# The next block's third and fourth W1 sums behind the second result of the block ahead

## The chip, the cores and the metric

The kernel runs on one core of one Trainium2 chip. What counts is the time of one execution on the device in microseconds (us). A core has five engines that run side by side, each working through its own instructions in their written order: PE (matrix products), DVE (elementwise work on vectors), ACT (activations and copies), POOL (here it mostly issues indirect DMAs, which gather and scatter rows) and SP (issues the plain DMAs). They wait for one another through semaphores.

## The reference

Attention over a causal window of 64 positions, then a mixture of experts in which each token goes through one expert's two matrix products.

```
B, H, S, D, E, F = 8, 8, 576, 512, 8, 1024      # D = 8 heads of 64
x = softmax(q k^T / 8 inside the window) v      # heads joined: (8, 576, 512)
logits = x @ w_gate;  local = sigmoid(x @ w_local)
for every sequence b, token s:
    e = argmax(logits) if s == 0 or local < 0.5 else the token before's e
    out[b, s] = softmax(logits[b, s])[e] * (relu(x[b, s] @ w1[e]) @ w2[e])
```

Everything is in 32-bit floats; there are 4608 tokens.

## The kernel before, in words

The first third computes attention and the gate. Then the tokens are sorted by expert into blocks, and the blocks are worked through one after another by `Experts.run`. A large block has 256 rows of one expert; the rows left over go into blocks of 128, 64 or 32 rows. The fixed order is: three early large blocks (-1, -2, -3), then 0, 1, a 128-row block, 2, a 32-row block, 3, a 128-row block, 4, 5, a 128-row block, 6, a 32-row block, 7, a 128-row block, 8, 9, a 64-row block, 10, 11, 12, and a last 64-row block.

From block -3 on, a large block's two matrix products (x by W1 in `big_hidden`, the result h by W2 in `big_result`) are each made as seven products of quarter matrices instead of eight, by Winograd's scheme. That takes sums of quarters ahead of the products: four sums of the left operand (`left`), four of the right one (`right`). For the first matrix product the left operand is W1 (tile `ws`, four sums of 128x1024 elements) and the right one x (tile `xs`). For the second it is h (`hs`) and W2 (again shown as `ws`). All of these sums run on DVE. In `left`, sum 2 needs sum 1, sum 4 needs sum 2, and sum 3 needs neither of them.

I number the seven products of a `big_result` R1 to R7 and those of a `big_hidden` H1 to H7, in the order in which PE runs them. Their PSUM tiles (`hp`) come from a pool of three buffers, and each product waits for whoever still reads its buffer. After R4, R5 and R6, DVE makes a quarter of the result from PSUM (`put`, line 1419). I call them the first, second and third put. The last quarter, after R7, is made by ACT. R7 adds onto the PSUM tile that the second put reads (`px`), so PE may not begin R7 before the second put has ended. H1 of the next block uses the buffer that the first put reads, and H2 the one that the third put reads.

In `run`, while PE is at R1 to R7 of one block, the DVE work for the next block has been written ahead of the puts: `turn` transposes the gathered rows, and `prepare` makes the four `xs` and the four W1 sums. H2 uses W1 sum 1, H3 sum 2, H5 sum 3 and H6 sum 4. In the stage this case is about, engines DVE, ACT, POOL, PE and SP all follow the written order. The hooks passed to `big_result` are called between the products; `step`, which most of them hold, has nothing left to do once the router's work is over, which is so before the places that change.

The third put is followed by the W2 sums of the next block (line 1320, written into a single buffer, so they wait for R7, which still reads the old ones), and on POOL by the scatter of the first half of the result (line 1488), behind which POOL has gathers for later blocks (line 1184). SP loads a block's W1 and W2 (line 1261) into a ring of four buffers, once PE and DVE are done with the old contents.

Of the kernel before, what the change touches and what calls it, by code (L numbers as in the profile page):

```python
# [42 lines left out]
FB = 3  # L43
# [131 lines left out]
def attention(ctx, tc, ring, kq, v3, v4, vt, vh, xs, lt, ok, wg, wg2, ident, rt, ex, small):  # L175
# [303 lines left out]
    for i, (sc, hp) in enumerate(units):  # L479
# [18 lines left out]
        if hp == 3 and sc not in GATED:  # L498
            turn(sc, x, 0)
            old = x  # L500
        elif sc and sc - 1 not in GATED:
            if hp == 0:
                turn(sc - 1, old, 1)
            elif hp == 2:
                logits(sc - 1, turned)
# [207 lines left out]
class Router:  # L713
# [70 lines left out]
    @staticmethod  # L784
    def last(ap):
        return ap.rearrange("p (c o) -> p c o", o=1)
# [5 lines left out]
    def gate(self, part, psum):  # L792
# [36 lines left out]
        for i in range(2):  # L829
# [55 lines left out]
                               Alu.add, Alu.add)  # L885
        base = tl("base", P, E * CMAX)[:, :E * n].rearrange("p (e c) -> p e c", e=E)
        vec.tensor_tensor(base, run, te, op=Alu.subtract)
        yield 1.9 if part else 1.2, False
        cnt = self.cnt[part]
# [270 lines left out]
def quarters(t, rows, cols):  # L1160

    r, c = rows // 2, cols // 2
    return [[t[:, i * r:(i + 1) * r, j * c:(j + 1) * c] for j in range(2)] for i in range(2)]


class Experts:
# [98 lines left out]
    def begin(self):  # L1265
        self.jobs = [self.fetch(-1)]

    def turn(self, st, quiet, later=False):
        while any(x is st for x, _ in self.asks):
            self.ask()  # L1270
        nc, n = self.nc, st["rows"]
        a = slice(HF, HF + n) if "quarter" in st else slice(n)
        st["xt"] = xt = self.xtp.tile([P, DK, BIG], F32, name="xt")
        for i, x in enumerate(st["x"]):
            o = xt[:, :, i * P:(i + 1) * P]
            if st["plain"]:
                tp = self.ps_t.tile([P, DK, P], F32, name="tp")
                for kk in range(DK):
                    nc.tensor.transpose(tp[:, kk, :n], x[a, kk * P:(kk + 1) * P], self.ident[a, a])
                (nc.scalar.copy if quiet else nc.vector.tensor_copy)(o[:, :, :n], tp[:, :, :n])  # L1280
                continue
            first, parts = st["parts"][0], len(st["parts"])
            nc.vector.transpose(
                o[:, :, :n].rearrange("p j (m t) -> p m j t", m=parts),
                x[:, first * P:(first + parts) * P].rearrange("p (m j d) -> p m j d", m=parts, j=DK))
        if n < P:
            pws = st["pw"][0]
            st["pw"] = pw = self.wk.tile([P, 1], F32, name="pw")
            for i in range(P // n):
                nc.vector.tensor_copy(pw[i * n:(i + 1) * n], pws[a])  # L1290
        if st["fast1"] and not quiet and not later:
            self.prepare(st)

    def prepare(self, st):

        st["xq"] = quarters(st["xt"], DK, BIG)
        st["xt"] = self.right("xs", st["xq"])
        w = quarters(st["w1"], DK, F)

        st["wq"] = [[w[0][0], w[1][0]], [w[0][1], w[1][1]]]  # L1300
        st["ws"] = self.left("ws1", st["wq"])

    def left(self, name, a):

        sub, add = Alu.subtract, Alu.add
        s1, s2, s3, s4 = self.sums(name, a)
        for o, x, y, op in ((s1, a[1][0], a[1][1], add), (s2, s1, a[0][0], sub), (s3, a[0][0], a[1][0], sub),
                            (s4, a[0][1], s2, sub)):
            self.nc.vector.tensor_tensor(o, x, y, op=op)
        return s1, s2, s3, s4  # L1310

    def right(self, name, b, marks=()):

# [18 lines left out]
    def halves(self, st):  # L1332

        hq = st["hq"]
        st["ha"] = [[hq[0][0], hq[1][0]], [hq[0][1], hq[1][1]]]
        st["hs"] = self.left("hs", st["ha"])

    def big_hidden(self, st, step):

# [244 lines left out]
    def run(self, ctx, rt, last=None):  # L1584

        tc = self.tc
        self.space(ctx)
        ps_r = ctx.enter_context(tc.tile_pool(name="ex_ps_r", bufs=1, space=PSUM))
        ctx.enter_context(tc.manual_schedule(engines={ET.PE, ET.SP}))
        rt.rows_of(ctx, tc, "rt_oh2", 3)  # L1590
        jobs = self.jobs

        def psum():
            return ps_r.tile([P, SC], F32, name="r")

        side = rt.second(psum)
        pause = 0.0

        def step():
            nonlocal side, pause  # L1600
            pause, trip = max(pause - STEP, -1.5), False
            while side and not trip and pause <= 0.0:
                w, trip = next(side, (0.0, None))
                pause += w + (0.6 if trip else 0.0)
                if trip is None:
                    side = None

        order = [-1 - n for n in range(FB)]
        between = [*range(NB, NB + SURE[1]), *range(KINDS[1] + 1, KINDS[1] + SURE[2])]
        quarters = list(range(KINDS[2], KINDS[2] + SURE[3]))  # L1610
        for n in range(SURE[0]):
            order.append(n)
            if n % 2 and between:
                order.append(between.pop(0))
            elif n % 4 == 2 and quarters:
                order.append(quarters.pop(0))
        order += between
        order.append(KINDS[1])
        assert not quarters
        jobs += [self.rows({}, order[1])] + [{"plain": True} for _ in range(2, FB)]  # L1620
        jobs[FB - 2]["later"] = True
        held = self.one.tile([1, 1], F32, name="held")
        self.nc.sync.dma_start(out=held, in_=jobs[1]["x"][1][:1, :1])
        for i, n in enumerate(order[1:FB]):
            self.weights(jobs[1 + i], n)
        self.turn(jobs[0], True)
        step()
        pause += 3.4
        for i, n in enumerate(order):
            quiet = i < FB  # L1630
            if i == FB - 1:
                while side and not rt.ready:
                    step()
                mark = last(self.ps_y.tile([P, D], F32, name="yp")) if last else None

                ctx.enter_context(tc.manual_schedule(engines={ET.PE, ET.SP, ET.DVE, ET.Activation, ET.Pool}))
                jobs.append(self.weights(self.rows({}, order[FB], True, True), order[FB]))
                jobs.append(self.weights({"plain": False}, order[FB + 1]))
                if jobs[i]["fast1"]:
                    self.prepare(jobs[i])  # L1640
            elif i >= FB:
                if i + 2 < len(order):
                    self.weights(jobs[i + 2], order[i + 2])
                if i + 3 < len(order):
                    jobs.append(self.rows({}, order[i + 3], paced=True))
            self.flush()
            if FB - 1 <= i < len(order) - 1:
                jobs[i]["later"] = True
            if n >= KINDS[2]:
                continue  # L1650
            if i == 1:
                pause += 4.5
            with tc.issue_after(mark.ins) if i == FB - 1 and mark else nullcontext():
                self.hidden(jobs[i], quiet, step, ((FK - 1, lambda: rt.links), (FK - 3, lambda: rt.links))[i] if i < 2 else None)
            if i + 2 < FB:
                self.rows(jobs[i + 2], order[i + 2], paced=True)
            if i == 1:
                rt.behind = jobs[1]["last"]
            if i == FB - 1:
                while side:  # L1660
                    step()
                self.rows(jobs[FB + 1], order[FB + 1], paced=True)
                jobs.append(self.rows({}, order[FB + 2], paced=True))
            if i + 1 == len(order):
                self.result(jobs[i], step)
                continue
            self.turn(jobs[i + 1], i + 1 < FB)
            if i + 2 < FB and jobs[i + 1]["fast1"]:
                self.prepare(jobs[i + 1])
            hooks = (step, ) * 6  # L1670
            if order[i + 1] >= KINDS[2]:
                one, turned, two = self.quarter(jobs[i + 1])
                after = jobs[i + 2]
                hooks = (lambda: None), one, turned, two, (lambda: self.turn(after, False, True)), \
                    (lambda: self.prepare(after))
            self.result(jobs[i], step, hooks)
# [64 lines left out]
```

## Time and profile before

| what | value |
|---|---|
| median of 3 runs | 633.9 us (629.37 to 635.15) |
| the profiled execution | 631.83 us, its span 630.1 us |
| PE busy | 604.0 us (96%) |
| DVE busy | 402.1 us (64%) |
| POOL busy | 275.5 us (44%) |
| ACT busy | 200.7 us (32%) |
| PE's waits for a put (line 1419) | 2.0 us in 6 waits |

The trace gives each instruction's start and length on its engine, and before an idle stretch the instruction that ended it. PE's matmuls are pipelined, so one starts before the former has ended; the distance from one start to the next is what a product takes.

### The profile page before, as it was taken

Reading aid. Unit: us, or ns where it says so; the run is one execution under the profiler, and the core shown is the slowest. Engines: PE = TensorE matmul, PEld = TensorE weight load, DVE = VectorE, ACT = ScalarE, POOL = GpSimd, SP = SyncE. Lnnn points to the kernel's source line nnn. Section 1 sums busy time; section 2 is a strip of 40 time slices with the busy share of each in tenths; the row PEclk is TensorE's granted clock in tenths of the full one; section 3 lists DMA queues with packets and bytes.
Section 4 is the critical chain, followed back from the end, with each engine's and each line's share of the span. In section 5 each row is a group of like instructions: output and inputs, shape, how many; then the busy total and the mean of one; then the engine's idle time right before and its main releaser. Section 6 shows DMA issues by size and latency. Waiting matters only on the chain. (4 is left out here: it accounts for less than half of the span.)

```text
span 630.1 us, 15072 instructions
## 1 busy us (share of the span) xinstructions
PE 604.0 (96%) x6253; PEld 530.7 (84%) x6253; DVE 402.1 (64%) x757; ACT 200.7 (32%) x368; POOL 275.5 (44%) x261
## 2 busy tenths in 40 slices
PE   8897988999999999999999999999999999999995
PEld 7676766788889998979898889888997998989994
DVE  5667569888986867346472785183927753886730
ACT  3756655632482131203130213022211221213120
POOL 4532111532103567448165873174375765462001
PEclk9999999999999999999999999999999999999998
DMA  8999898886945566487966765678678656965501
GB/s 319 397 419 400 326 377 298 287 319 238 384 154 202 185 227 250 165 295 248 403 244 236 304 221 208 225 305 318 284 262 320 225 186 240 374 217 208 197 18 39
DMA packets 31880, 165.80 MB, mean 263 GB/s; under 512 B 10531, under 2 KB 12217, under 8 KB 22586
## 3 DMA queue, kind: packets, MB, share of 16 engines
q1 hardware_dynamic: 20394, 135.54, 57.9%
q0 software_dynamic: 11408, 29.20, 13.0%
q8 instruction: 51, 0.84, 0.5%
q14 instruction: 27, 0.22, 0.1%
HBM read 145.52 MB, written 19.59 MB: 262 GB/s over the span
## 5 line engine op out<-in xcount | busy, mean ns | idle before, releaser
L1184 POOL DMA_INDIRECT xg<-xs,g x118 | 139.1, 1179 | 46.5 <-issue 25.6
L1488 POOL DMA_INDIRECT out_dram<-y,idx x36 | 40.8, 1133 | 159.0 <-DVE y L1419 69.9
L1408 PE MATMUL hp<-ws,hs 128*128 128x256 f32 x384 | 88.9, 380 | 0.0
L1408 PEld LDWEIGHTS hp<-ws,hs 128*128 128x128 f32 x384 | 72.6, 190 | 10.9 <-issue 1.2
L1357 PE MATMUL hp<-xs,ws 128*128 128x128 f32 x672 | 79.7, 275 | 0.0
L1357 PEld LDWEIGHTS hp<-xs,ws 128*128 128x128 f32 x672 | 77.3, 192 | 0.1
L1508 PE MATMUL hp<-xt,w 128*64 128x64 f32 (+2 forms) x640 | 66.2, 276 | 0.0
L1508 PEld LDWEIGHTS hp<-xt,w 128*128 128x128 f32 (+1 forms) x640 | 60.8, 170 | 4.1 <-issue 0.7
L1419 DVE SCALAR_TENSOR_TENSOR y<-hp,pws,kept 128x256 f32<-128x256 f32 x48 | 22.1, 480 | 63.5 <-issue 38.1
L1408 PE MATMUL hp<-w,h 128*128 128x256 f32 x256 | 60.5, 379 | 0.0
L1369 DVE TENSOR_TENSOR h<-hp,keep 128x512 f32<-128x512 f32 x42 | 28.6, 690 | 44.0 <-PE hp L1357 43.2
L1357 PEld LDWEIGHTS hp<-xt,w 128*128 128x128 f32 x448 | 53.2, 192 | 2.7 <-issue 2.3
L1357 PE MATMUL hp<-xt,w 128*128 128x128 f32 x448 | 54.7, 275 | 0.0
L394 PEld LDWEIGHTS sp<-w 64*64 64x64 f32 x1296 | 39.9, 139 | 16.1 <-issue 11.5
L1408 PEld LDWEIGHTS hp<-w,h 128*128 128x128 f32 x256 | 47.3, 190 | 5.7
L394 PE MATMUL sp<-w 64*64 64x128 f32 (+1 forms) x1296 | 45.8, 272 | 5.7 <-issue 4.2
L425 ACT ACTIVATE p<-sp 128x512 f32<-128x512 f32 x72 | 39.1, 595 | 37.6 <-PE sp L394 35.2
L440 PE MATMUL xo<-vb,p 128*64 128x74 f32 (+1 forms) x576 | 45.0, 230 | 5.5 <-DVE x L450 2.2
L430 DVE TENSOR_TENSOR p<-p,mask 128x1024 f32<-128x1024 f32 x29 | 35.6, 1227 | 22.6 <-ACT p L425 22.5
L1184 POOL DMA_INDIRECT pws<-xw,gx x40 | 43.7, 1093 | 13.1 <-issue 9.8
L440 PEld LDWEIGHTS xo<-vb,p 128*64 128x64 f32 x576 | 39.2, 139 | 9.7 <-issue 4.0
L1320 DVE TENSOR_TENSOR ws<-w 128x1024 f32<-128x1024 f32 x32 | 39.1, 1224 | 11.5 <-PE hp L1408 9.6
(287 smaller groups left out, 967.3 us busy)
## 6 DMA issues: line engine op xcount, KB each, us to landing
w<-in_w_dram SPq DMA_DIRECT2D x22, 2048.0 KB, 9.4
w<-in_w1t_dram SPq DMA_DIRECT2D x20, 2048.0 KB, 8.9
w<-in_kq_dram SPq DMA_DIRECT2D x17, 1024.0 KB, 10.4
w<-in_w_dram SPq DMA_DIRECT2D x24, 512.0 KB, 8.3
xs<-x POOLq DMA_DIRECT2D x9, 1024.0 KB, 7.0
va<-in_v_dram SPq DMA_DIRECT2D x5, 1184.0 KB, 5.3
vtt<-in_vt_dram SPq DMA_DIRECT2D x5, 1024.0 KB, 6.3
va<-in_v_dram SPq DMA_DIRECT2D x3, 1040.0 KB, 14.2
```

Of the source, the lines that this page charges most:

```text
L394: nc.tensor.matmul(sp[j][c * WIN:(c + 1) * WIN, a:b], lhsT=kt[h, hp, block * WIN:(block + 1) * WIN], rhs=qt[h, hp, a:b], start=not biased, ...
L425: nc.scalar.activation(p[:, j], sp[j], Act.Exp, scale=DH ** -0.5)
L430: masked.append(nc.vector.tensor_tensor(p, p, m.to_broadcast([P, 2, SC]), op=Alu.mult))
L440: nc.tensor.matmul(xo[par * WIN:(par + 1) * WIN, j, s * VW:s * VW + n], lhsT=p[:, j, b * WIN:(b + 1) * WIN], rhs=w[:, s, 2 * hp + j, :n], ...
L1184: return self.nc.gpsimd.indirect_dma_start(out=out, out_offset=None, in_=table[:rows, :], in_offset=bass.IndirectOffsetOnAxis(ap=idx, axis=0))
L1320: self.nc.vector.tensor_tensor(o, x, y, op=sub)
L1357: mm = nc.tensor.matmul(out[:, m, :], lhsT=a[:, kk, m * P:(m + 1) * P], rhs=b[:, kk, :], start=start and m + kk == 0, stop=stop and (m, kk ...
L1369: nc.vector.tensor_tensor(o, x, y, op=add)
L1408: mm = nc.tensor.matmul(out, lhsT=a[:, m, :], rhs=b[:, m, :], start=start and m == 0, stop=stop and m == FK // 2 - 1, skip_group_check=True)
L1419: nc.vector.scalar_tensor_tensor(o, x, pw[i], y2, Alu.mult, Alu.add)
L1488: return self.nc.gpsimd.indirect_dma_start(out=self.out[:, :], out_offset=bass.IndirectOffsetOnAxis(ap=st["idx"][:, s:s + 1], axis=0), in_ ...
L1508: mm = nc.tensor.matmul(hp[a, i, :], lhsT=st["w1"][:, kk, m * P:(m + 1) * P][:, a], rhs=st["xt"][:, kk, :n], start=(kk == 0), stop=(kk == ...
```

## The change

`left` can now stop after two of its four sums and hand back a function that makes the rest. `prepare` and `turn` pass it on. In `run`, where the block at hand is large and the next block is at or past the fourth of the order, that function becomes the fifth hook of `big_result`, which is called behind the second put. Where the next block isn't a large one, nothing differs.

```
-    def turn(self, st, quiet, later=False):
+    def turn(self, st, quiet, later=False, rest=False):
...
         if st["fast1"] and not quiet and not later:
-            self.prepare(st)
+            return self.prepare(st, rest)
-    def prepare(self, st):
+    def prepare(self, st, rest=False):
...
-        st["ws"] = self.left("ws1", st["wq"])
+        st["ws"], later = self.left("ws1", st["wq"], rest)
+        return later
-    def left(self, name, a):
+    def left(self, name, a, rest=False):
         sub, add = Alu.subtract, Alu.add
         s1, s2, s3, s4 = self.sums(name, a)
-        for o, x, y, op in ((s1, a[1][0], a[1][1], add), (s2, s1, a[0][0], sub), (s3, a[0][0], a[1][0], sub),
-                            (s4, a[0][1], s2, sub)):
-            self.nc.vector.tensor_tensor(o, x, y, op=op)
-        return s1, s2, s3, s4
+        todo = [(s1, a[1][0], a[1][1], add), (s2, s1, a[0][0], sub), (s3, a[0][0], a[1][0], sub), (s4, a[0][1], s2, sub)]
+        def make(n):
+            for o, x, y, op in todo[:n]:
+                self.nc.vector.tensor_tensor(o, x, y, op=op)
+            del todo[:n]
+        make(2 if rest else 4)
+        return (s1, s2, s3, s4), lambda: make(4)
...
-            self.turn(jobs[i + 1], i + 1 < FB)
+            more = self.turn(jobs[i + 1], i + 1 < FB, rest=i + 1 >= FB and jobs[i]["fast2"])
...
-            hooks = (step, ) * 6
+            hooks = (step, ) * 4 + (more or step, step)
```

In the order of the run a large block stands directly behind a large one, with the later of the two at or past the fourth, at six places: -3 to 0, 0 to 1, 4 to 5, 8 to 9, 10 to 11 and 11 to 12. No instruction is added or removed, and none moves on PE, ACT, POOL or SP. On DVE, at the place 0 to 1, the order before was the following. `ws_3341<-w` and its like on line 1309 are the W1 sums of block 1, `y` on line 1419 the three puts of block 0, and `ws_3408` on line 1320 the W2 sums of block 1.

```order
L1309 TENSOR_TENSOR ws_3341<-w 128x1024
L1309 TENSOR_TENSOR ws_3341<-ws_3341,w 128x1024
L1309 TENSOR_TENSOR ws_3341<-w 128x1024
L1309 TENSOR_TENSOR ws_3341<-w,ws_3341 128x1024
L1419 SCALAR_TENSOR_TENSOR y<-hp,pws,kept_3356 128x256
L1419 SCALAR_TENSOR_TENSOR y<-hp,pws,kept_3363 128x256
L1419 SCALAR_TENSOR_TENSOR y<-hp,pws,kept_3370 128x256
L1320 TENSOR_TENSOR ws_3408<-w 128x1024
L1320 TENSOR_TENSOR ws_3408<-w,ws_3408 128x1024
```

The same stretch of DVE after the change (six lines further down in the file for the puts and the W2 sums, three for the W1 sums):

```order
L1312 TENSOR_TENSOR ws_3341<-w 128x1024
L1312 TENSOR_TENSOR ws_3341<-ws_3341,w 128x1024
L1425 SCALAR_TENSOR_TENSOR y<-hp,pws,kept_3354 128x256
L1425 SCALAR_TENSOR_TENSOR y<-hp,pws,kept_3361 128x256
L1312 TENSOR_TENSOR ws_3341<-w 128x1024
L1312 TENSOR_TENSOR ws_3341<-w,ws_3341 128x1024
L1425 SCALAR_TENSOR_TENSOR y<-hp,pws,kept_3368 128x256
L1326 TENSOR_TENSOR ws_3408<-w 128x1024
L1326 TENSOR_TENSOR ws_3408<-w,ws_3408 128x1024
```

Sums 3 and 4 have moved from in front of the first two puts to between the second and the third. At the place -3 to 0, where block 0 is the first large block that is gathered the later way, the piece before and the piece after read:

```order
L1309 TENSOR_TENSOR ws_3172<-w 128x1024
L1309 TENSOR_TENSOR ws_3172<-ws_3172,w 128x1024
L1309 TENSOR_TENSOR ws_3172<-w 128x1024
L1309 TENSOR_TENSOR ws_3172<-w,ws_3172 128x1024
L1419 SCALAR_TENSOR_TENSOR y<-hp,pws,kept_3187 128x256
L1419 SCALAR_TENSOR_TENSOR y<-hp,pws,kept_3194 128x256
L1419 SCALAR_TENSOR_TENSOR y<-hp,pws,kept_3201 128x256
```

And now, with the same names:

```order
L1312 TENSOR_TENSOR ws_3172<-w 128x1024
L1312 TENSOR_TENSOR ws_3172<-ws_3172,w 128x1024
L1425 SCALAR_TENSOR_TENSOR y<-hp,pws,kept_3185 128x256
L1425 SCALAR_TENSOR_TENSOR y<-hp,pws,kept_3192 128x256
L1312 TENSOR_TENSOR ws_3172<-w 128x1024
L1312 TENSOR_TENSOR ws_3172<-w,ws_3172 128x1024
L1425 SCALAR_TENSOR_TENSOR y<-hp,pws,kept_3199 128x256
```

The move is the same here; the other four places read like these two.

More of the change, by code (lines that the diff above doesn't have):

```diff
@@ L1335, in halves @@
         st["ha"] = [[hq[0][0], hq[1][0]], [hq[0][1], hq[1][1]]]
-        st["hs"] = self.left("hs", st["ha"])
+        st["hs"], _ = self.left("hs", st["ha"])
     def big_hidden(self, st, step):
```

## The prediction, made before the result was known

> **What bounds the kernel now.** I read the page first, then PE's waits, then windows over the stretches that change, then the timelines of PE and DVE there.
>
> ```profile
> PE 604.0 (96%) x6253; PEld 530.7 (84%) x6253; DVE 402.1 (64%) x757; ACT 200.7 (32%) x368; POOL 275.5 (44%) x261
> PE hp L1408 <- DVE y L1419: 2.0, 6, 0.4
> PE hp L1357 <- DVE h L1369: 0.4, 2, 0.2
> ```
>
> The first row is the page's busy time, the others are from the list of waits (total us, times, longest). PE is busy for 604.0 of 630.1 us, so only its waits are for sale. In the expert stage there are two kinds: six waits for a put (line 1419, the result quarters that DVE makes), and two small ones for the hidden-layer adds, at blocks that the change doesn't touch. So the change can win no more than the waits for a put cost.
>
> What they cost is more than 2.0 or less, depending on where they lie. These windows run from the start of R1 to the start of the next block's first product. The columns are length; busy us and count for PE, PEld, DVE, ACT, POOL; the granted clock; DMA share; GB/s.
>
> ```profile
> 207.01:219.09 12.08, 12.08 (x58) 10.64 (x57) 10.18 (x16) 1.42 (x3) 7.44 (x6) 1.00 0.66 215
> 231.60:244.36 12.76, 12.36 (x59) 10.56 (x57) 11.06 (x17) 2.02 (x4) 10.02 (x10) 1.00 0.66 220
> 256.86:268.95 12.09, 12.09 (x58) 10.65 (x57) 4.46 (x8) 2.02 (x4) 4.32 (x5) 1.00 0.63 204
> 363.54:376.20 12.66, 12.36 (x59) 10.56 (x57) 10.96 (x17) 2.02 (x4) 9.82 (x9) 1.00 0.66 219
> 495.33:507.99 12.66, 12.36 (x59) 10.56 (x58) 10.96 (x17) 2.02 (x4) 10.22 (x9) 1.00 0.67 214
> 552.62:565.26 12.64, 12.36 (x59) 10.56 (x58) 10.94 (x17) 2.02 (x4) 9.26 (x8) 1.00 0.65 217
> 577.76:590.40 12.64, 12.36 (x59) 10.56 (x57) 10.94 (x17) 2.02 (x4) 0.99 (x1) 1.00 0.57 189
> ```
>
> The third is a large block with a small one behind it, where the change does nothing and PE never idles: seven products take 12.09 us. The other six are the six places of the change. The first of them (-3 to 0) takes 12.08 and loses nothing. The five others take 12.76, 12.66, 12.66, 12.64 and 12.64. That they are the five, and that the sixth of the six waits lies outside the change, also follows from here: the idle in these windows is length less PE busy, 0.40 + 0.30 + 0.30 + 0.28 + 0.28 = 1.56 us, and 0.44 of the 2.0 is left for another place. DVE is busy for about 11 of 12.7 us in them: over these stretches it is nearly the bound.
>
> **The change part by part.** What it removes. PE's and DVE's timelines at the place 0 to 1 (start, length, and in brackets the idle before it and who ended it):
>
> ```profile
> 238.51 1.89 PE L1408 MATMUL hp<-ws,hs 128*128 128x256 f32 x8
> 240.24 1.89 PE L1408 MATMUL hp<-w,hs 128*128 128x256 f32 x8
> 242.53 1.99 PE L1408 MATMUL hp<-ws,h 128*128 128x256 f32 x8 [0.40 <-DVE y L1419]
> 244.36 1.95 PE L1357 MATMUL hp<-xt,w 128*128 128x128 f32 x16
> 246.14 3.74 PE L1357 MATMUL hp<-xs,ws 128*128 128x128 f32 x32
> 251.50 1.95 PE L1357 MATMUL hp<-xs,ws 128*128 128x128 f32 x16
> ...
> 236.94 1.21 DVE L1309 TENSOR_TENSOR ws<-w 128x1024 f32<-128x1024 f32 x1
> 238.19 1.23 DVE L1309 TENSOR_TENSOR ws<-ws,w 128x1024 f32<-128x1024 f32 x1
> 239.33 1.22 DVE L1309 TENSOR_TENSOR ws<-w 128x1024 f32<-128x1024 f32 x1
> 240.47 1.22 DVE L1309 TENSOR_TENSOR ws<-w,ws 128x1024 f32<-128x1024 f32 x1
> 241.60 1.26 DVE L1419 SCALAR_TENSOR_TENSOR y<-hp,pws,kept 128x256 f32<-128x256 f32 x3
> 244.56 1.23 DVE L1320 TENSOR_TENSOR ws<-w 128x1024 f32<-128x1024 f32 x1 [1.70 <-PE hp L1408]
> 251.77 0.69 DVE L1369 TENSOR_TENSOR h<-hp,keep 128x512 f32<-128x512 f32 x1 [2.40 <-PE hp L1357]
> ```
>
> The PE rows are R5, R6, R7, H1, H2 with H3, and H5. DVE is still at sums 3 and 4 when R4 and R5 are done, so all three puts run together from 241.60. The second ends at about 241.60 + 0.40 + 0.48 = 242.48, and R7 starts at 242.53; undisturbed it would start 1.73 behind R6, at 241.97. The next block's first product then comes 0.67 late (12.76 - 12.09).
>
> With the change DVE reaches the first put at 239.33, where sum 3 was. The second put must wait for R5. How soon a put follows its product, where DVE is free, is seen at an undisturbed block:
>
> ```profile
> 265.50 1.89 PE L1408 MATMUL hp<-w,hs 128*128 128x256 f32 x8
> 267.23 1.89 PE L1408 MATMUL hp<-ws,h 128*128 128x256 f32 x8
> 265.75 0.48 DVE L1419 SCALAR_TENSOR_TENSOR y<-hp,pws,kept 128x256 f32<-128x256 f32 x1 [1.24 <-PE hp L1408]
> ```
>
> That is 0.25 behind the start of R6, so at place 0 to 1 the second put would run from 240.49 to 240.97, a whole 1.0 us ahead of R7 at 241.97. The first put (239.33 + 0.48 = 239.81) is out of its way. The four other places have the same lengths on both engines, so all five waits go.
>
> The sum by lengths: 0.67 + 0.57 + 0.57 + 0.55 + 0.55 = **2.91 us** (each window less 12.09). By idle alone it would be 1.56 us. I take 2.91, since a product's start behind a wait is late by more than the idle: the weight load isn't hidden there. The rows for that at the same place, and for R7's matmuls:
>
> ```profile
> 242.53 1.59 PEld L1408 LDWEIGHTS hp<-ws,h 128*128 128x128 f32 x8 [0.80 <-DVE y L1419]
> L1408 PE MATMUL hp<-ws,h x128: 379/379/483, 162.1 to 614.8; 128*128 128x256 f32 x128
> ```
>
> The weight load starts with the matmul instead of ahead of it, and the longest matmul is 483 ns instead of 379. The Trainium skill bears on this: "TensorE: Matmul & The Clock Gate", section Single matmul latency, has a single matmul cost some 166 ns more than one in a stream at full clock, since its drain isn't hidden. An estimate by that page is 1.56 + 5 x 0.166 = 2.39 us, between the two ends; the windows show more, and the measurement decides. The granted clock is 1.00 in all the windows, so nothing is to be had from the clock.
>
> What it moves. Two sums at each of six places, 1.22 us each (1.14 from start to start), now stand in front of the third put. Counted from R6's start: second put at 0.25, sum 3 at 0.65 (puts follow one another 0.40 apart), sum 4 at 1.79, third put from 2.92 to 3.40. Before, it ended at 242.86, 2.62 behind R6; so it ends 0.78 later on the clock, and 0.78 + 0.67 later against PE, which is now earlier. Who waits for it:
> - H2, whose PSUM buffer it reads. H2 starts 1.73 + 1.72 + 1.79 = 5.24 behind R6 (R7, H1, and the step from 244.36 to 246.14). The cover is 5.24 - 3.40 = **1.84 us**. If that were gone, each further us would be a us of PE.
> - The W2 sums behind it on DVE. They wait for R7 anyway: at 244.56, 0.20 behind H1's start, so at 3.45 + 0.20 = 3.65. DVE is free at 3.32; the cover is 0.33 us, and behind it lie the 2.40 us for which DVE idles before the first add at 251.77. That add stays on time.
> - The scatter of the first half on POOL, and the gathers behind it:
>
> ```profile
> 245.31 1.36 POOL L1488 DMA_INDIRECT out_dram<-y,idx  x1 [0.30 <-issue]
> 375.90 1.01 POOL L1488 DMA_INDIRECT out_dram<-y,idx  x1 [0.30 <-issue]
> 589.18 0.99 POOL L1488 DMA_INDIRECT out_dram<-y,idx  x1 [13.78 <-DVE y L1419]
> 598.83 0.98 POOL L1488 DMA_INDIRECT out_dram<-y,idx  x1 [8.66 <-issue]
> ```
>
> At 245.31 POOL comes to the scatter 2.4 us after the put's old end and 1.7 after its new one (240.24 + 3.40 = 243.64). At 375.90 it came from other work; there the put would end at about 375.6, no delay worth naming. At 589.18 POOL does wait for the put, and goes 0.8 later, with nothing behind it for 8.66 us. Cost nothing.
> - The sums' own users: sum 3 is first needed by H5, at 251.50, sum 4 behind it; both are done by 243.3. Cost nothing. The first two sums stay where they were, and H1's buffer comes free earlier.
>
> The sums issue no DMA. SP's loads into the W1 ring come behind the last product that reads the tile, far later than sum 4, so no transfer is moved by the sums themselves. At -3 to 0, where nothing waits, the third put ends about 0.9 later (3.40 against 217.64 + 0.48 - 215.64 = 2.48 behind R6), under the same cover of 1.84: zero.
>
> ```profile
> 215.64 1.89 PE L1408 MATMUL hp<-w,hs 128*128 128x256 f32 x8
> 217.64 0.48 DVE L1419 SCALAR_TENSOR_TENSOR y<-hp,pws,kept 128x256 f32<-128x256 f32 x1 [0.83 <-PE hp L1408]
> ```
>
> The profiled execution: 631.83 - 2.91 = 628.92 us.
>
> **The rivals.**
>
> *Nothing is gained (10%).* PE is earlier at five places, and something that was just in time is now late by as much: a gather or a weight load, which become PE's or DVE's next wait. For it: POOL is busy for 9 to 10 us in four of the windows, DVE for 11. Against it: POOL's gathers and SP's loads are released by PE's own progress, which moves too, and PE has no wait for a DMA in this stage. DVE has two that name one:
>
> ```profile
> DVE y L1419 <- DMA pws<-xw,gx: 1.2, 1, 1.2
> DVE y L1419 <- DMA xg<-xs,g: 1.2, 1, 1.2
> ```
>
> Both are in front of a put and as long as the 1.24 us in front of the undisturbed put above, which waited for its product; so the product came last there too. Time: 631.83 by the profiled execution, 0.5% from my forecast.
>
> *Slower: the third put comes so late that H2 waits (3%).* The moved sums now lie beside POOL's run of gathers and its scatter. If a sum were held up for the whole of one POOL instruction, it would begin that much later.
>
> ```profile
> L1309 DVE TENSOR_TENSOR ws<-w x28: 1211/1218/1264, 181.9 to 585.4; 128x1024 f32<-128x1024 f32 x28
> L1309 DVE TENSOR_TENSOR ws<-w,ws x14: 1209/1218/1219, 185.4 to 586.5; 128x1024 f32<-128x1024 f32 x14
> L1184 POOL DMA_INDIRECT xg<-xs,g x118: 939/954/1975, 209.2 to 566.2; - x118
> ```
>
> The longest gather took 1.975 us. Two sums held by one each put the third put 3.95 us later; it decides from 1.84 on, so H2 is late by 2.11 at each of six places: 6 x 2.11 - 2.91 = +9.7, 641.6 us. Against it: among gathers all along, no W1 sum took over 1.264 us; it is the gathers that vary, from 0.939 to 1.975. The Trainium skill has such a rule ("SBUF — State Buffer", section Who interferes with whom): a Vector instruction with two SBUF inputs and a GpSimd instruction that reads SBUF exclude each other, and whichever starts first holds the other off for its whole length. These rows show no sum held off so.
>
> *The waits shrink but stay (5%).* If the second put's end is seen by PE later than I count, or DVE arrives later at sum 1 than in this trace, part of the idle stays. Half of it gives 631.83 - 1.46 = 630.4. It would take more than the 1.0 us between the put's end and R7.
>
> **How the numbers follow.** The forecast has 82%. The profiled execution's 631.83 lies 2.07 below the median of the three timed runs, 633.9, and inside their spread. I take the middle of all four executions, (631.83 + 633.9) / 2 = 632.87, as the time before, and less 2.91 it is **630.0 us**. The range: the fastest run less the gain, 629.37 - 2.91 = 626.5, and the slowest with no gain, 635.2. That takes in the bound by idle alone (1.56), the half and the nothing; the slower rival is outside.
>
> One per cent, 6.3 us, is about what a measurement of this kernel can tell from no change, and the three runs themselves span 5.8. The forecast is a gain of 0.46%, and the waits for a put hold no more. So within 1% gets 0.84. Faster by over 1% can only come from where the runs fall, the forecast being 0.6% below the median of 633.9: 0.13. Slower by over 1% is the slower rival: 0.03.
>
> **What would show it.** Right: in PE's list of waits, line 1408 for a put falls from 2.0 us in 6 to about 0.44 in one; the windows over R1 to R7 are 12.1 us at all six places; the span is some 2.9 us shorter; the third put ends about 3.4 us behind R6's start, and the first W2 sum starts 0.2 behind H1. Wrong: a wait of H2 (line 1357 of before) for a put, W1 sums longer than 1.3 us, or a wait of DVE for gathered rows. The forecast falls if the windows shorten and the span doesn't.

## The result, and the profile after

| | before | after |
|---|---|---|
| median | 630.7 us, 22 runs (627.65 to 635.15) | 626.61 us, 22 runs (625.2 to 632.61) |
| the profiled execution | 631.83 us | 627.78 us |
| its span | 630.1 us | 626.0 us |

The ratio is **0.995**, with a 95% interval of 0.9933 to 0.9966: the change gains between 2.1 and 4.2 us, half a per cent. Runs over 1.5% above the fastest of their kernel are left out of the ratios here and below, among them four of the first kernel's first twelve and one of 879.18 us of the last kernel's six.

These are the page's busy row and PE's waits in the expert stage after the change (total us, times, longest). The lines have moved down by six: 1414 is the result's products, 1425 the puts, 1363 and 1375 the hidden layer.

```profile
PE 600.5 (96%) x6253; PEld 528.9 (84%) x6253; DVE 403.2 (64%) x757; ACT 200.5 (32%) x368; POOL 271.4 (43%) x261
PE hp L1363 <- DVE h L1375: 0.5, 2, 0.2
PE hp L1414 <- DVE y L1425: 0.4, 1, 0.4
```

Of the six waits for a put, 2.0 us, one of 0.4 is left. The two waits for an h add are still there. The windows from R1's start to H1's start at the six places, columns as in the prediction:

```profile
206.68:218.77 12.09, 12.09 (x58) 10.65 (x57) 10.27 (x16) 1.42 (x3) 6.99 (x6) 1.00 0.65 216
231.28:243.37 12.09, 12.09 (x59) 10.64 (x58) 11.11 (x17) 2.02 (x4) 9.35 (x10) 1.00 0.70 226
362.55:374.64 12.09, 12.09 (x59) 10.64 (x57) 11.04 (x17) 2.02 (x4) 9.05 (x8) 1.00 0.71 231
493.82:505.90 12.08, 12.08 (x58) 10.64 (x57) 11.04 (x17) 2.02 (x4) 9.64 (x9) 1.00 0.71 231
550.54:562.63 12.09, 12.09 (x59) 10.64 (x58) 11.03 (x17) 2.02 (x4) 8.56 (x9) 1.00 0.70 227
575.13:587.22 12.09, 12.09 (x58) 10.64 (x57) 11.03 (x17) 2.02 (x4) 0.00 (x0) 1.00 0.58 194
```

In each of them PE is busy for the whole length. The timelines of PE and DVE at the place 0 to 1, where the prediction did its working, show how (start, length, idle before it and who ended it):

```profile
239.91 1.89 PE L1414 MATMUL hp<-w,hs 128*128 128x256 f32 x8
241.64 1.89 PE L1414 MATMUL hp<-ws,h 128*128 128x256 f32 x8
243.37 1.95 PE L1363 MATMUL hp<-xt,w 128*128 128x128 f32 x16
245.15 3.74 PE L1363 MATMUL hp<-xs,ws 128*128 128x128 f32 x32
...
237.83 1.23 DVE L1312 TENSOR_TENSOR ws<-ws,w 128x1024 f32<-128x1024 f32 x1
238.97 0.48 DVE L1425 SCALAR_TENSOR_TENSOR y<-hp,pws,kept 128x256 f32<-128x256 f32 x1
240.17 0.48 DVE L1425 SCALAR_TENSOR_TENSOR y<-hp,pws,kept 128x256 f32<-128x256 f32 x1 [0.72 <-issue]
240.57 1.22 DVE L1312 TENSOR_TENSOR ws<-w 128x1024 f32<-128x1024 f32 x1
241.70 1.22 DVE L1312 TENSOR_TENSOR ws<-w,ws 128x1024 f32<-128x1024 f32 x1
242.84 0.48 DVE L1425 SCALAR_TENSOR_TENSOR y<-hp,pws,kept 128x256 f32<-128x256 f32 x1
243.57 1.23 DVE L1326 TENSOR_TENSOR ws<-w 128x1024 f32<-128x1024 f32 x1 [0.25 <-PE hp L1414]
250.78 0.69 DVE L1375 TENSOR_TENSOR h<-hp,keep 128x512 f32<-128x512 f32 x1 [2.40 <-PE hp L1363]
```

The PE rows are R6, R7, H1 and H2 with H3. The second put starts 0.26 behind R6 and is through at 240.65, a whole 0.99 us ahead of R7. The third put ends at 243.32, which is 3.41 behind R6 and 1.83 ahead of H2; at the five other places it ends 3.40 or 3.41 behind R6. The first W2 sum starts 0.20 behind H1, and DVE still idles for 2.40 us ahead of the first h add.

**Where in the span the time went.** The first row of each pair begins the expert stage's region that I use from here on (the router's last transposes, ahead of all six places), the second is PE's last product, the third the last scatter. Before, and then after:

```profile
200.15 0.59 PE L1022 MATMUL r<-t,ident 128*32 128x54 f32 x32 [0.16 <-DVE t L1017]
618.87 3.63 PE L1538 MATMUL yp<-w,h 128*64 128x256 f32 x32
623.29 0.98 POOL L1546 DMA_INDIRECT out_dram<-y,idxh  x1 [4.48 <-ACT y L1543]
```

```profile
199.83 0.59 PE L1022 MATMUL r<-t,ident 128*32 128x54 f32 x32 [0.16 <-DVE t L1017]
615.69 3.63 PE L1544 MATMUL yp<-w,h 128*64 128x256 f32 x32
620.11 0.98 POOL L1552 DMA_INDIRECT out_dram<-y,idxh  x1 [4.49 <-DVEq L143]
```

From the first row to the second is 418.72 us before and 415.86 after: 2.86 gained where the change is. The other 1.24 of the span's 4.1 lie outside it: 0.32 ahead of the first row, and 0.92 between the last scatter's start and the span's end (6.81 before, 5.89 after).

### The profile page after: what moved, and what is told of

The parts are those of the page before. It is cut to its first block, busy times and chain, and to the rows that moved or that the text cites. A ratio compares the mean times of both kernels' runs of the same rounds, so it can differ in the third digit from the quotient of the medians.

```text
span 626.0 us, 15072 instructions
## 1 busy us (share of the span) xinstructions
PE 600.5 (96%) x6253; PEld 528.9 (84%) x6253; DVE 403.2 (64%) x757; ACT 200.5 (32%) x368; POOL 271.4 (43%) x261
## 5 line engine op out<-in xcount | busy, mean ns | idle before, releaser
L1184 POOL DMA_INDIRECT xg<-xs,g x118 | 134.2, 1138 | 46.0 <-issue 25.3
L1376 ACT ACTIVATE h<-h 128x512 f32<-128x512 f32 x42 | 26.3, 630 | 60.1 <-DVE h L1375 60.1
```

The costliest lines, as they stand in the source:

```text
L1184: return self.nc.gpsimd.indirect_dma_start(out=out, out_offset=None, in_=table[:rows, :], in_offset=bass.IndirectOffsetOnAxis(ap=idx, axis=0))
L1376: nc.scalar.activation(o, x if y is None else o, Act.Relu)
```

## The experiments

I call the theory of the prediction *the gate*: PE stands still only where the second put ends after R7 is due, or the third after H2 is due, and what DVE does otherwise is free. The rival to it is that DVE's load or the mere length of its queue sets the time. The yardstick beside the ratio is the region from the two rows above, which leaves out the stage ahead and the end of the program. It repeats within 0.1 us between kernels that should agree (table at the end of this section).

**Only the fourth sum moved.** One sum fewer ahead of the puts is 1.14 us; each wait is 0.28 to 0.40.

```
-        make(2 if rest else 4)
+        make(3 if rest else 4)
```

> Only the fourth W1 sum goes behind the second put; the third stays in front of the first. Theory (the gate: PE loses what the second put ends later than R7's due time, and nothing else counts): with one sum less in front, DVE reaches the first put 1.14 us earlier, the second put ends 1.1 us behind R6's start at the latest, R7 is due at 1.73, so all five waits go and the time is that of the change, 0.995 of before (about 627 us). Rival (the load: what counts is how much DVE work is taken from in front of the puts): half the work moved, half the gain, 0.9975. In the trace: one wait of R7 for a put left (0.4 us, at the early block) by the first, several by the second.

> Only the fourth sum behind the second put, on the chip of this call. Theory of the gate (one sum fewer ahead of the puts is 1.14 us, each wait is 0.28 to 0.40 us): all five waits go, 0.995, one wait for a put of 0.4 us left in the trace. Rival (half of the moved work gives half of the gain): 0.9975.

It ran on two chips. The first was a slower one: the kernel before took 643.83 us there. The ratios are 0.9914 (0.9871 to 0.9956) there, and **0.9958** (0.9932 to 0.9984) on the other chip. DVE at the place 0 to 1 in the second run, with PE's waits for DVE in the expert stage:

```profile
239.41 1.22 DVE L1312 TENSOR_TENSOR ws<-w 128x1024 f32<-128x1024 f32 x1
240.54 0.87 DVE L1425 SCALAR_TENSOR_TENSOR y<-hp,pws,kept 128x256 f32<-128x256 f32 x2
241.33 1.22 DVE L1312 TENSOR_TENSOR ws<-w,ws 128x1024 f32<-128x1024 f32 x1
```

```profile
PE hp L1414 <- DVE y L1425: 0.4, 1, 0.4
PE hp L1363 <- DVE h L1375: 0.4, 2, 0.2
```

The first two puts run together and end at 241.41; R7 starts on time at 242.14. All five waits are gone with half of the move, and the region is 415.81, the same as with the whole of it. The third sum's move is margin. The rival's 0.9975 lies inside the second interval, so it is the waits and the region of that run that exclude it.

**Three sums moved.** `make(1)` in the same place.

> Sums 2, 3 and 4 go behind the second put, only sum 1 stays in front. Gate: the third put ends 4.55 us behind R6's start, H2 is due at 5.24, so 0.7 of the cover of 1.84 is left; the W2 sums start at 4.5 instead of 3.65 and still end 1.5 us ahead of the first add. Time as the change, 0.995. Load: one and a half times the gain, 0.9925.

The ratio is 0.9947 (0.9913 to 0.9981), as the gate has it. The rival's 0.9925 lies inside the interval too; on that slower chip the regions can't decide, since PE has waits of up to 1.30 us there, for ACT above all, that the faster chips' traces don't have.

**All four moved.** `make(0)`: by the working of the prediction the third put then ends 5.8 behind R6, past the 5.24 at which H2 is due.

> All four W1 sums go behind the second put. Gate: the third put ends 0.25 + 0.40 + 1.25 + 3 x 1.14 + 0.48 = 5.8 us behind R6's start, H2 is due at 5.24 and waits some 0.6 us for its buffer, at all six places, also at -3 to 0; with the exposed weight load about 0.7 each, 4.2 us over the change: 1.002 of before. In the trace six waits of H2 for a put. Load: twice the gain, 0.990.

The ratio is 0.9953 (0.9916 to 0.999): neither. The third put came as late as computed, but no H2 waited for it. DVE and PE at the place 0 to 1:

```profile
244.47 0.48 DVE L1425 SCALAR_TENSOR_TENSOR y<-hp,pws,kept 128x256 f32<-128x256 f32 x1
...
239.15 1.89 PE L1414 MATMUL hp<-w,hs 128*128 128x256 f32 x8
244.38 3.74 PE L1363 MATMUL hp<-xs,ws 128*128 128x128 f32 x32
```

The put ends 5.80 behind R6. H2 starts 5.23 behind it, before the put has even begun to read its buffer, so H2 cannot be writing that buffer. The built program says the same: where the third put is written behind four sums, the pool gives H2 the buffer that R7 has left, and the third put's goes to H4. This holds for three sums, too. At the place 11 to 12 the trace shows whom H2 waits for now. ACT, which makes the last quarter from R7's buffer, was late there for a reason that isn't shown, and H2 starts 0.06 behind its end, 577.86; the third put had ended at 577.23:

```profile
577.39 0.47 ACT L1447 ACTIVATE y<-hp,pws 128x256 f32<-128x256 f32 x1 [8.68 <-PE hp L1363]
577.92 3.84 PE L1363 MATMUL hp<-xs,ws 128*128 128x128 f32 x32 [1.09 <-ACT y L1447]
```

So here the pool, not the gate, was what I had left out, and the test of the gate was still to be made.

**The three buffers written down by hand.** First with the change as it is, then with all four sums moved, so that H2 always uses the third put's buffer.

```
-        pz, py, px = (self.ps_h.tile([P, n, P], F32, name="hp") for _ in range(3))
+        pz, py, px = (self.ps_h[i].tile([P, n, P], F32, name="hp") for i in range(3))
...
-        px, py, pz = (self.ps_h.tile([P, D], F32, name="hp")[:, :w] for _ in range(3))
+        px, py, pz = (self.ps_h[i].tile([P, D], F32, name="hp")[:, :w] for i in range(3))
...
-        self.ps_h = ctx.enter_context(tc.tile_pool(name="ex_ps_h", bufs=3, space=PSUM))
+        self.ps_h = [ctx.enter_context(tc.tile_pool(name=f"ex_ps_h{i}", bufs=1, space=PSUM)) for i in range(3)]
```

> The change, with the three PSUM buffers of the large blocks' products written down by hand (each product always in the same one of three, H2 always in the one that the third put reads). Both theories: nothing waits that did not wait, so as the change, 0.995 (0.993 to 0.997); one wait for a put, 0.4 us, in the trace. If it is slower, PE's list of waits names the product whose buffer comes free too late.

> The same fixed buffers, and all four W1 sums behind the second put at the six places, so that the third put ends some 5.8 us behind R6, 0.6 behind the time at which H2 is due (5.24). Theory of the cover (the third put gates H2 once it ends later than 5.24, and in the kernel with four sums moved this was only hidden because H2 got another buffer): six waits of H2 for a put, 0.4 to 0.7 us each, some 0.7 us of PE at each place, 4.2 us over the kernel with fixed buffers alone: about 1.002. Rival (the third put gates nothing, whichever the buffer): 0.995, no wait of H2 for a put.

Fixed buffers alone: 0.9932 (0.9907 to 0.9957), region 415.77. With four sums moved: **1.0025** (0.9999 to 1.0052), region 420.12, so 4.35 more. PE's waits of that kernel for a put, and its PE and DVE at the place 0 to 1:

```profile
PE hp L1363 <- DVE y L1425: 2.7, 6, 0.5
```

```profile
240.06 1.89 PE L1414 MATMUL hp<-w,hs 128*128 128x256 f32 x8
241.79 1.89 PE L1414 MATMUL hp<-ws,h 128*128 128x256 f32 x8
243.52 1.95 PE L1363 MATMUL hp<-xt,w 128*128 128x128 f32 x16
245.92 3.84 PE L1363 MATMUL hp<-xs,ws 128*128 128x128 f32 x32 [0.45 <-DVE y L1425]
...
245.38 0.48 DVE L1425 SCALAR_TENSOR_TENSOR y<-hp,pws,kept 128x256 f32<-128x256 f32 x1
```

There are the six waits of H2. It starts at 245.92, as the put ends at 245.86, and 5.86 behind R6 instead of 5.24: 0.62 late, and 0.10 more for its own longer group (3.84 for 3.74). Six times 0.72 is 4.3 us, as expected. So the cover of 1.84 us that the prediction gave the third put is real, and behind it the loss (4.35) is more than the change gains (2.86).

**Sums 3 and 4 behind the third put** (the sixth hook instead of the fifth).

```
-            hooks = (step, ) * 4 + (more or step, step)
+            hooks = (step, ) * 5 + (more or step, )
```

> Sums 3 and 4 go behind the third put instead of in front of it. The third put then ends 2.46 us behind R6 instead of 3.40, and the W2 sums start at 4.65 instead of 3.65, both covered. Gate: the same time as the change, 0.995, within 0.001. Rival (the later third put costs something that the waits don't show, by POOL's scatter and the gathers behind it): faster than the change, by up to the 0.8 us of delay at each of six places, 0.988 to 0.993.

0.9946 (0.9915 to 0.9977), the same gain as the change's within the noise. The rival's 0.988 to 0.993 reaches into the interval, so the time doesn't settle it. What speaks against it is that with the change all six windows already have the 12.08 or 12.09 us of undisturbed products, so they have nothing left to give; a gain elsewhere isn't excluded.

**The move at the first place only** (-3 to 0, where nothing waited before).

```
-            ... rest=i + 1 >= FB and jobs[i]["fast2"])
+            ... rest=i + 1 == FB and jobs[i]["fast2"])
```

> The move is made at -3 to 0 alone, where R7 didn't wait before; the other five places are as before. Gate: no gain, 1.000, and five waits of R7 for a put of 0.28 to 0.40 us stay, with the early one 2.0 us in 6. Load: a sixth of the gain, 0.999, which the time can't tell; the trace decides: by the load the seven products at -3 to 0 get shorter than 12.08 us.

1.0005 (0.9985 to 1.0025), region 418.64. PE's list keeps every wait:

```profile
PE hp L1414 <- DVE y L1425: 2.0, 6, 0.4
```

The seven products at -3 to 0 take 12.09 us, for 12.08 before. So the move costs and gains nothing where no put was late.

**The order of before, with the third sum made twice** at the six places.

```
-        make(2 if rest else 4)
-        return (s1, s2, s3, s4), lambda: make(4)
+        if rest:
+            todo.insert(3, todo[2])
+        make(9)
+        return (s1, s2, s3, s4), lambda: make(9)
```

> The order of before, with the third W1 sum made twice at each of the six places, so DVE comes 1.14 us later to the puts. Gate: at the five places every bit of it is lost, 5 x 1.14 = 5.7 us; at -3 to 0 the second put ended 0.56 us ahead of R7 and now ends 0.58 behind it, some 0.7 us with the exposed weight load. Together 6.4 us, 1.010 of before, in the trace six waits of R7 of 1.4 to 1.5 us at five places and 0.4 to 0.5 at the first. Rival (the waits are covered further on, DVE idles 2.4 us ahead of the hidden-layer adds): 1.000 to 1.004.

1.0103 (1.0077 to 1.0129), region 425.86, so 7.14 more than before. PE's waits for a put, and R7 at 0 to 1:

```profile
PE hp L1416 <- DVE y L1427: 8.8, 7, 1.6
```

```profile
237.68 2.48 DVE L1312 TENSOR_TENSOR ws<-w 128x1024 f32<-128x1024 f32 x2
242.13 2.00 PE L1416 MATMUL hp<-ws,h 128*128 128x256 f32 x8 [1.54 <-DVE y L1427]
```

R7's idle grows from 0.40 to 1.54 here and by 1.26 to 1.32 at the four other places, and at the sixth, -3 to 0, it is now 0.59. That is 6.83 us more of idle in all, and with 0.27 for the new wait (the price worked out below) and 0.05 for one of the h adds 7.15, for the 7.14 of the region. The 6.4 expected was too low because it took 1.14 for the repeated sum: the row of both shows it start 2.48 - 1.22 = 1.26 behind the first. What stands in front of the puts is paid in full.

**The order of before, with the second put read by ACT.** ACT scales R5's result out of PSUM, and DVE adds the kept part later, where PE waits for nothing.

```
+            if (i, j) == (1, 1) and st.get("by_act"):
+                nc.scalar.activation(o, x, Act.Copy, scale=pw[i])
+                nc.vector.tensor_tensor(o, o, y2, op=Alu.add)
+                return
...
+            jobs[i]["by_act"] = i + 1 >= FB and jobs[i]["fast2"] and jobs[i + 1]["fast1"]
```

> The order of the sums as before, but at the six places ACT reads the second put's PSUM tile (0.47 us), and DVE adds the kept part from SBUF later, where the second put was. R7 then waits for ACT, which is idle there, and no longer for DVE: done 0.72 us behind R6's start, R7 due at 1.73. Gate: the gain of the change with no sum moved, 0.995, the five waits gone. Rival (the gain comes from DVE reaching the first and third put earlier, or from another effect of the new order): no gain, 1.000.

0.9954 (0.994 to 0.9969), region 415.76, one wait for a put of 0.4 left. All four W1 sums still stand ahead of the puts, and DVE is as busy as before; still the gain is that of the change. So it is R7's wait for its buffer that was worth this much, not DVE's order as such.

**The two h adds as well.** The change, and the fourth W2 sum of blocks 3 and 7 made behind the h sums.

```
-        self.prepare2(st)
+        last = self.prepare2(st, (), st.get("split"))
...
+        if last:
+            last()
...
+                after["split"] = True
```

> The change, and at blocks 3 and 7 (behind a 32-row block), where H7 waits for a hidden-layer add because DVE is late with eight sums, the fourth W2 sum goes behind the four sums of h; R7 alone needs it. Gate: DVE reaches the adds 1.14 us earlier, H7's two waits of 0.24 us go, with the exposed weight load 0.5 us each; 1.0 us less than the change, 0.9935 of before. Rival (the h sums or the next transposes come later and cost as much): 0.995.

0.9936 (0.9918 to 0.9954). The rival's 0.995 lies inside the interval; the region decides: it is 414.84, 1.02 less than with the change. PE's list for a put or an h add has one wait left:

```profile
PE hp L1423 <- DVE y L1434: 0.4, 1, 0.4
```

**And the last wait for a put**, which lies in block -1, ahead of the region: that kernel, with the put in question read by ACT.

> The kernel with the last W2 sum later, and besides the second put of the shared expert's last block read by ACT, where PE's one wait for a put is left (0.44 us idle). If ACT is free there: that wait is gone, and some 0.7 us of PE with it (the idle and 0.27, as at the other places): 0.9925 against the kernel before. Rival: the time is lost beside it again, at what follows the block: 0.9936, as the kernel with the last W2 sum later alone.

R1, R7 and the next block's first product in the kernel with the two h adds, and the same three in this one:

```profile
148.34 1.89 PE L1423 MATMUL hp<-w,h 128*128 128x256 f32 x8
159.31 2.00 PE L1423 MATMUL hp<-ws,h 128*128 128x256 f32 x8 [0.44 <-DVE y L1434]
161.15 13.98 PE L1523 MATMUL hp<-xt,w 128*128 128x256 f32 x64
```

```profile
149.51 1.89 PE L1423 MATMUL hp<-w,h 128*128 128x256 f32 x8
159.87 1.89 PE L1423 MATMUL hp<-ws,h 128*128 128x256 f32 x8
161.59 13.98 PE L1527 MATMUL hp<-xt,w 128*128 128x256 f32 x64
```

12.81 us become 12.08, and the step from R1 to the region's start falls from 49.02 to 48.30: the 0.7 expected, and nothing lost beside it, as the region is 414.90. The ratio, 0.9898 (0.9857 to 0.9938), rests on five runs; its interval holds 0.9925 but doesn't tell it from 0.9936. At 624.7 us, the median of the five, this is the lowest of them all, and by the trace it has no wait of a large block's products for DVE left.

The regions side by side, worked out from the same two rows of each trace as above:

| kernel | waits of PE removed (-) or added (+) | region, us |
|---|---|---|
| before | | 418.72 |
| first place only | none | 418.64 |
| the change | - five for the second put | 415.86 |
| only the fourth sum | - the same five | 415.81 |
| second put by ACT | - the same five | 415.76 |
| fixed buffers | - the same five | 415.77 |
| last W2 sum later | - the same five, two for an h add | 414.84 |
| fixed buffers, four sums moved | - the same five, + six of H2 | 420.12 |
| third sum twice | + 1.14 to 1.32 on five, a sixth of 0.59 | 425.86 |

## Why the prediction was right, point by point

**The five waits and their price.** It said 2.91 us from the windows' lengths, and not the 1.56 us of idle. The region gives 2.86, which is 2.91 less the 0.05 by which one of the two h adds' waits grew (0.24 and 0.19 before, 0.24 each after). The price of a wait for DVE is its idle and 0.27 us more: (2.91 - 1.56) / 5 = 0.27. The other runs give the same: the two h adds, (415.86 - 414.84 - 2 x 0.24) / 2 = 0.27; the early put, 0.73 - 0.44 = 0.29; the six waits of H2, (4.35 - 2.7) / 6 = 0.28. By the rows at the place 0 to 1 the 0.27 has two parts. Undisturbed, R7 starts 0.16 ahead of R6's end (1.89 - 1.73); behind the wait this overlap is lost on top of the idle. And from R7 to H1 it is 1.83 instead of 1.73, as much more as the longest matmul takes over the others (483 for 379 ns). R7's weight load starts with it there, whereas after the change it starts 0.22 ahead of R7 at 241.64:

```profile
241.42 1.70 PEld L1414 LDWEIGHTS hp<-ws,h 128*128 128x128 f32 x8
```

H2 with fixed buffers and four sums moved splits alike, 0.62 - 0.45 = 0.17 and 0.10. That the late weight load makes the 0.10 is read from these rows and not tested; and the ends of PE's rows are modelled by the profile, so the split hangs on them, the windows' lengths don't.

The Trainium skill ("TensorE: Matmul & The Clock Gate", section Single matmul latency) gives 166 ns as the constant part of a single bf16 matmul's latency at full clock. The first part, 0.16 to 0.17, is as large; the estimate by it alone, 2.39 us in all, lacks the second part and is less than the windows and the regions show.

**The covers.** The third put's end, 3.41 behind R6 for 3.40, the W2 sum at 0.20 behind H1, and the 2.40 of idle ahead of the h add came as worked out. That the cover of 1.84 decides is shown by the fixed buffers with four sums moved, and only by them.

**The rivals.** *Nothing is gained*: no wait took the place of the five; POOL, SP and ACT end none of PE's waits in the expert stage after the change. *Waits shrink but stay*: none stayed, at any of the five. *Slower*, by sums that a gather holds off: these are the W1 sums after the change, among them the twelve that were moved.

```profile
L1312 DVE TENSOR_TENSOR ws<-w x28: 1211/1219/1225, 181.5 to 584.4; 128x1024 f32<-128x1024 f32 x28
L1312 DVE TENSOR_TENSOR ws<-w,ws x14: 1212/1218/1222, 185.1 to 585.6; 128x1024 f32<-128x1024 f32 x14
```

None took over 1.225 us, beside gathers in five of the six windows (in the sixth POOL has nothing to do). The Trainium skill's rule on exclusive ports ("SBUF — State Buffer", section Who interferes with whom) would hold a sum off for a gather's whole length if the instruction that issues the gather reads SBUF through the shared ports; no run here shows that.

**What was off.** The time, 630.0 for 626.61, which is inside the range by 0.1 us only; that it fell inside is luck. The term that failed is the time before. I took 632.87, the middle of four executions; the 22 runs beside the kernel after have 630.7, which is 2.2 of the 3.4 us. The remaining 1.2 is the gain: 4.1 us by the medians, for the sum of 2.91. By the ratio, 0.995, the gain is 3.2 us, and the region explains 2.9. The interval, 2.1 to 4.2, holds all three, so it can't be told whether there is more. In the profiled executions the excess, 0.32 and 0.92, lies ahead of and behind everything that the change touches. The prediction had nothing wrong on the buffers for the change itself, but its statement that each further us of the third put would be a us of PE holds only while the pool keeps giving H2 the third put's buffer.

## What to carry to other kernels

Price a wait of PE by the length of the window against an undisturbed one, not by its idle: here each cost 0.27 us more than the idle shown. Look for the one instruction in another engine's queue that PE waits for, and for what stands ahead of it; work moved behind it is free as far as the next such instruction's cover reaches, and no further. Where a pool hands out the buffers, a moved reader can also move who waits for it, so look up the buffers again before costing a longer move.

## What was not expected of the hardware

Between kernels that remove the same waits the region repeats within 0.1 us in some 416, while the stage ahead of it does not: its end, the region's start, lies between 196.71 and 200.33 us in the ten profiled executions on the faster chips, and the stretch from the last scatter's start to the span's end between 5.71 and 6.87. So the spread of the timed runs, as far as these profiles show it, comes from outside the stretch under study.

The chip of the first four kernels was slower, 643.83 us against 630 for the same kernel before. The regions of the three kernels read there are 427.69 to 431.03 us, with the same start (198.51 to 200.07): the time is lost in the expert stage. Single stalls stand there at places that the change doesn't touch, such as this one of DVE, at the third h add of block 4, from the run of the kernel with the fourth sum moved on that chip:

```profile
366.89 0.69 DVE L1375 TENSOR_TENSOR h<-hp,keep 128x512 f32<-128x512 f32 x1 [3.31 <-PE hp L1363]
```

The instruction itself takes its usual 0.69 us, but DVE stands idle for 3.31 us before it; the two adds ahead of it had 1.26 and 1.09. ACT, which works on what the add writes, is idle for 3.37 and starts at 367.62, just behind the add's end at 367.58. What held the add isn't shown, and no experiment was made on it.
